# Attention with two banks for the transposes: the next scores go behind one transpose

## The chip, the cores and the metric

One NeuronCore of a Trainium2 chip runs the whole program. The metric is the device time of one execution in microseconds: the median of the runs before the change is 971.01 us (970.05 to 972.16, three runs).

## The reference

The program is three layers after each other, on float32 data. Only the first is touched by the change: attention with queries averaged in twos.

```python
# q, k, v: 4 x 8 heads x 1152 x 64
q_pool = q.reshape(B, H, S // 2, 2, D).mean(axis=3)          # 576 queries
scores = scale * np.matmul(q_pool, k.transpose(0, 1, 3, 2))  # 576 x 1152
scores = scores - np.max(scores, axis=-1, keepdims=True)
attn = np.exp(scores)
attn = attn / (np.sum(attn, axis=-1, keepdims=True) + 1e-09)
out = np.matmul(attn, v)
# then two gated layers of width 512 and 1024 over 4 x 576 rows (moe, moe2)
```

## The kernel before, in words

Attention works on 16 pairs of heads. A pair has 2 x 576 queries, cut into nine tiles of 128 rows: four whole tiles of each head and one mixed tile of the two rests of 64. The main loop (L630) has one turn, here called a place, for each tile; places are numbered 0 to 8 in a pair. In place s the program issues the exponential of tile s + 1, brings tile s of exponentials into the layout that the product with the values wants (keys on partitions), computes the scores of tile s + 2, and their maximum. The scores (`scores`, L286) are six matmuls of 128 x 384 into three PSUM banks of one of two buffers SC, the mixed tile nine (two 64 rows wide or fed by `qc`). The maximum (`smax`, L307) is one reduction on DVE, the exponential (`sexp`, L322) one ACTIVATE on ACT with the row sums as a second, small instruction. So SC[s % 2] passes from scores to maximum to exponential, and only then are its banks free.

There are two ways to turn a tile of exponentials, in pairs 1 to 14 (`quick`):
- Places 0 to 3, here called block places (`by_block`): one 32 x 32 block transpose on DVE into the tile BLK (`turn_blocks`, L361); after the fourth, 16 DMAs on the SP queue move the blocks into the tile E (`move_blocks`, L367). These are the near queries, 256 of each head.
- Places 4 to 8, here called turned places: nine 128 x 128 transposes on PE (`tfill`, L337). Six go into banks 1 and 2 of the tile's own scores buffer, which its exponential has just set free, three into a bank TX. Copies (`tcopy`, L391) bring them to the tile M, two of 384 columns on ACT and one on DVE. These are the far queries, 320.

Pairs 0 and 15 turn all nine tiles on PE. The value products (`pv_part`, L400) have a PSUM bank of their own, tag `pv`, and stand where the table `shares` (L346) puts them: it lists (place, number of key blocks), counted from the pair's place 0, so place 9 is place 0 of the next pair. The near products of an inner pair stand in places 8 and 9, the far ones in 10, 11 and 12. A float32 matmul of these shows in the trace as two instructions.

What else the engines do stands in tables of places as well. PREP lists POOL's cuts of q and k of the next pair into a high and a low part (`q_sum`, `q_own`, `k_hi`, `k_lo`), q's copy to the other half of the partitions on ACT (`q_double`), and the loads. The weights of the next layers come as 64-bit floats, 21 pieces in all, one in an even inner pair, two in an odd one; a piece goes through `conv_steps` (L107): load (SP), Abs (ACT, `mag`), clamp (POOL), three steps on the bits (DVE), high part (ACT), low part (POOL), store (SP). BITS says where the DVE steps stand. A step is recorded at one of three hooks of a place: `at_gap` (its start), `at_mid` (before the scores), `at` (its end). Each engine, and the SP queue, works in the order in which the program is written.

Of the kernel before, what the change touches and what calls it, by code (L numbers as in the profile page):

```python
# [11 lines left out]
F32 = mybir.dt.float32  # L12
F32R = mybir.dt.float32r
# [49 lines left out]
def attn_moe_kernel(ctx: ExitStack, tc: tile.TileContext, qT, kT, vP, muk, mur, wk, wv, wr, wth, wtr, wti, wch, ident, out):  # L63
# [94 lines left out]
    def attention(first):  # L158
# [97 lines left out]
        def k_hi(P):  # L256
            khs[P] = nat.tile([128, S], F32R, tag="kh", name="kh")
            cut_hi("pool", khs[P], raws[P])

        def k_lo(P, h, i):  # L260
            c = slice(SP * i, SP * i + SP)
            d, o = half[h], half[1 - h]
            if i == 0:
                t = kts[P, h] = kp.tile([128, S], F32R, tag="kt", name="kt")
                cut_hi("pool", t[d], raws[P][d])
            cut_lo("pool", kts[P, h][o, c], raws[P][d, c], khs[P][d, c])
# [124 lines left out]
        def tcopy(n, c):  # L391
            e = ("act", "act", "dve")[c] if quick(n // KT) else COPY[3 if n == 0 else 4 if n in (2, 4) else 2 if n % 18 in SHORT else n % 2][c]
            out = erow(n, c)
# [4 lines left out]
            bank(e, r, b)  # L398

        def pv_part(k, x):  # L400
# [106 lines left out]
        def start():  # L507
# [108 lines left out]
        assert next(pieces, None) is None  # L616
# [565 lines left out]
```

## Time and profile before

| what | value |
|---|---|
| median of three runs | 971.01 us |
| profiled execution | 972.1 us, span 970.3 us |
| PE busy | 922.6 us, 95% of the span |
| DVE, ACT, POOL busy | 691.5, 550.8, 612.8 us |
| attention's inner pairs (1 to 14) | about 38 to 446 us |
| granted PE clock, mean | 0.995 |

A time in the trace is counted from the start of the span. A row of the timeline may merge several instructions of one kind (x6), and its duration runs from the first one's start to the last one's end; ends of matmuls overlap the next start. What an engine can do is therefore best read from start to start.

### The profile page before, as it was taken

The numbers are of one execution on the slowest core, as the hardware profiler recorded it, in microseconds if no ns is written. First come the engines' busy times: TensorE is split into PE (matmuls) and PEld (weight loads), VectorE is DVE, ScalarE is ACT, GpSimd is POOL, SyncE is SP. The second block draws the span as 40 slices with busy tenths as digits, with TensorE's granted clock in tenths as the row PEclk, the third lists the DMA queues.
The fourth block names the chain that finished last, engine by engine and source line by source line (L and its number), as shares of the span: only waits on it lengthen the run. The fifth ranks groups of instructions, "written<-read, shape, count | busy, mean of one in ns | idle before, by whom it ended". The sixth has DMA issues, their size and how long they took to land.

```text
span 970.3 us, 17479 instructions
## 1 busy us (share of the span) xinstructions
PE 922.6 (95%) x6328; PEld 780.8 (80%) x6328; DVE 691.5 (71%) x974; ACT 550.8 (57%) x1131; POOL 612.8 (63%) x663
## 2 busy tenths in 40 slices
PE   7988999999999998998999899999999999999998
PEld 5766666666666666666898899999999999999998
DVE  6787888877888887784538888888646764575722
ACT  6767766677666668765556555646435433343410
POOL 7767877687786777773417556556536665574731
PEclk9999999999999999999999999999999999999999
DMA  8176757687575777645563333333402501010001
GB/s 260 56 205 166 221 194 224 191 269 205 164 225 184 236 209 229 181 126 156 187 212 105 101 103 95 99 94 122 161 2 98 185 2 50 1 44 7 25 26 49
DMA packets 60807, 132.65 MB, mean 137 GB/s; under 512 B 10736, under 2 KB 29872, under 8 KB 60720
## 3 DMA queue, kind: packets, MB, share of 16 engines
q1 hardware_dynamic: 60720, 131.53, 43.7%
q8 instruction: 50, 0.82, 0.4%
q14 instruction: 37, 0.30, 0.1%
HBM read 73.08 MB, written 24.79 MB: 101 GB/s over the span
## 4 chain that ended last, share of the span: by engine, by line
PE 59%; DVE 14%; ACT 9%; DMA 7%; SPq 5%; issue 3%; POOL 3%; DVEq 0%; ACTq 0%; POOLq 0%
PE ps L1074 12%; PE ps L826 9%; PE ps L807 9%; PE sc L297 6%; PE ps L1093 5%; PE pv L412 5%; PE ps L1020 5%; DVE m L318 5%; ACT e L330 5%; SPq L374 4%; PE sc L340 3%; PE ps L776 3%; DVE cv L141 2%; DVE blk L365 2%; ACT q L254 2%
## 5 line engine op out<-in xcount | busy, mean ns | idle before, releaser
L318 DVE TENSOR_REDUCE m<-sc 128x1 f32<-128x1152 f32 x138 | 186.1, 1348 | 66.6 <-PE sc L297 65.5
L330 ACT ACTIVATE e<-sc,m 128x1152 f32<-128x1152 f32 x144 | 176.2, 1224 | 71.3 <-DVE m L318 70.0
L297 PE MATMUL sc<-kt,q 128*128 128x384 f32 (+1 forms) x864 | 200.6, 358 | 8.1 <-ACT M L397 3.7
L297 PEld LDWEIGHTS sc<-kt,q 128*128 128x128 f32 (+1 forms) x864 | 142.1, 187 | 39.0 <-issue 19.8
L1074 PE MATMUL ps<-b,a 128*128 128x288 f32 x816 | 111.3, 296 | 0.0
L1074 PEld LDWEIGHTS ps<-b,a 128*128 128x128 f32 x816 | 109.4, 188 | 0.6
L807 PE MATMUL ps<-x,a 128*128 128x288 f32 x768 | 103.7, 295 | 2.5 <-DVE xt L831 2.5
L807 PEld LDWEIGHTS ps<-x,a 128*128 128x128 f32 x768 | 102.2, 188 | 2.8 <-DVE xt L831 2.7
L826 PE MATMUL ps<-k,b 128*128 128x288 f32 x768 | 103.4, 294 | 0.0
L826 PEld LDWEIGHTS ps<-k,b 128*128 128x128 f32 x768 | 102.0, 188 | 0.3
L340 PEld LDWEIGHTS sc<-idn,e 128*128 128x128 f32 x528 | 58.2, 143 | 49.2 <-ACT e L330 38.5
L340 PE MATMUL sc<-idn,e 128*128 128x128 f32 x528 | 78.2, 285 | 19.8 <-ACT e L330 19.8
L200 POOL TENSOR_TENSOR kt<-kn,kh 64x576 fp32r<-64x576 f32 (+1 forms) x64 | 90.6, 1436 | 2.2
L412 PE MATMUL pv<-M,vn 128*64 128x320 f32 x576 | 87.4, 440 | 0.0
L365 DVE STREAM_TRANSPOSE blk<-e 128x1152 f32<-128x1152 f32 x56 | 76.0, 1357 | 0.0
L412 PE MATMUL pv<-E,vn 128*64 128x256 f32 x576 | 70.3, 388 | 3.5 <-DMA E<-blk 3.1
L794 POOL TENSOR_TENSOR k<-h,k 128x288 fp32r<-128x288 f32 x64 | 56.7, 900 | 18.7 <-ACT k L793 17.4
L412 PEld LDWEIGHTS pv<-M,vn 128*64 128x64 f32 x576 | 37.4, 136 | 36.1 <-issue 11.3
L412 PEld LDWEIGHTS pv<-E,vn 128*64 128x64 f32 x576 | 39.6, 138 | 27.4 <-issue 10.0
L810 DVE TENSOR_TENSOR h<-h 128x288 f32<-128x288 f32 x64 | 38.1, 601 | 26.9 <-ACT h L809 26.6
L1038 ACT ACTIVATE q<-q 128x512 f32<-128x512 f32 x18 | 11.4, 632 | 79.3 <-DVE q L1035 79.3
L149 POOL TENSOR_TENSOR a<-a 128x192 fp32r<-128x192 f32 (+1 forms) x29 | 20.6, 709 | 56.5 <-ACT a L145 28.4
(138 smaller groups left out, 1747.6 us busy)
## 6 DMA issues: line engine op xcount, KB each, us to landing
E<-blk SPq DMA_DIRECT2D x224, 144.0 KB
vn<-vP SPq DMA_DIRECT2D x16, 576.0 KB
kn<-kT SPq DMA_DIRECT2D x15, 576.0 KB
qn<-qT SPq DMA_DIRECT2D x15, 576.0 KB
b<-wtk SPq DMA_DIRECT2D x9, 576.0 KB
rb<-scr SPq DMA_DIRECT2D x32, 144.0 KB
out<-xt SPq DMA_DIRECT2D x32, 144.0 KB
cv<-wk SPq DMA_DIRECT2D x8, 512.0 KB
```

Source lines behind the costliest of these rows:

```text
L200: engines[e].tensor_tensor(out, x, hi.bitcast(F32), ALU.subtract)
L297: r = pe.matmul(sc[0:m, c, 0:384], lhsT=x, rhs=k[:, 384 * c:384 * c + 384], start=(i == 0), stop=(i == len(ops) - 1),)
L318: r = dve.tensor_reduce(m, scs[n][:, :, 0:384], axis=AX.XY, op=ALU.max, negate=True)
L330: r = act.activation(e, sc[:, :, 0:384], AF.Exp, bias=m, scale=1.0, accum_out=rss[P][:, t:t + 1])
L340: r = pe.transpose(ps[:, 128 * j:128 * j + 128], es_[n][:, c, 128 * j:128 * j + 128], idn)
L365: dve.transpose(out, es_[n].rearrange("p a b -> p (a b)").rearrange("p (k m i) -> p k m i", k=KT, m=4))
L412: pe.matmul(out, lhsT=vns[P][:, h, j], rhs=e, start=(x == 0), stop=(x == KT - 1))
L794: pool.tensor_tensor(q[:, 1], h, q[:, 0].bitcast(F32), ALU.subtract)
L807: pe.matmul(ps, lhsT=WK[k, f // 4][:, w, 128 * (f % 4):128 * (f % 4) + 128], rhs=x[k][:, c], start=(k == 0 and n == 0), stop=(k == 3 and n ...
L826: pe.matmul(pss[d], lhsT=WV[f][:, w, 128 * d:128 * d + 128], rhs=k2[f][:, c], start=(f == 0 and n == 0), stop=(f == 7 and n == 2))
L1020: pe.matmul(ps, lhsT=y[k // 2][:, k % 2, x], rhs=WT[k][:, w], start=(k == 0 and p == 0), stop=(k == 3 and p == 2))
L1074: pe.matmul(pss[d], lhsT=zs[j][z][:, 128 * d:128 * d + 128], rhs=WTK[min(j, 8)][:, w, cs], start=(m == 0 and n == 0), stop=(m == 8 and n = ...
```

## The change

Transposes of the turned places go to two banks, TX and TY, and to bank 2 of the tile's scores buffer; TY is also the bank of the value products, which had `pv` before. Of a tile's nine key blocks, the last goes first, alone, into bank 2 ("o", copied by ACT); then come the scores of tile s + 2; then four blocks into TY ("y", copied by ACT at the start of the next place) and four into TX ("x", copied by DVE after the maximum). The tables of places change with it: value products in two near and two far parts, the bits of the weights in places 2 and 3, the preparation of q and k, Abs and the stores. An inner diff of the code and of one line of each table:

```diff
-PREP = ((0, 0, 'kh'), (0, 2, 'qs'), (0, 2, 'qo', 0), ..., (3, 1, 'qd', 0), ..., (3, 2, 'qd', 1), (4, 2, 'kl', 1, 0), (5, 1, 'kl', 1, 1), ...)
+PREP = ((-1, 2, 'qs'), (0, 0, 'qm'), (0, 0, 'qo', 0), ..., (2, 1, 'qd', 0), (2, 2, 'kt', 0), (3, 1, 'kt', 1), (3, 1, 'qd', 1), ..., (6, 2, 'kl', 1, 1), ...)
-BITS = (((8, 1), (8, 2), (9, 1)), ((2, 1), (3, 1), (8, 2)))
+PIECES = {"a": (((2, 1), (2, 2), (3, 1)), (9, 13, 15)), "b": (((3, 2), (11, 1), (11, 2)), (12, 14, 16)), "e": (((3, 1), (3, 1), (3, 2)), (9, 13, 15))}
...
+        TY = psV.tile([128, 512], F32, tag="ty", name="ty")
...
             if P == NP - 2:
-                return ((7, 2), (8, 7)), ((9, 5), (11, 4))
+                return ((8, 9),), ((9, 5), (11, 4))
...
-            return ((8, 4), (9, 5)), ((10, 3), (11, 3), (12, 3))
+            return ((9, 5), (10, 4)), ((11, 5), (12, 4))
...
+        FILL = {"o": (8, 9), "y": (0, 4), "x": (4, 8)}
+        def fill(n, w):
+            flat = es_[n].rearrange("p a b -> p (a b)")
+            k0, k1 = FILL[w]
+            ps = {"o": scs[n][:, 2], "x": TX, "y": TY}[w]
+            for j, k in enumerate(range(k0, k1)):
+                r = pe.transpose(ps[:, 128 * j:128 * j + 128], flat[:, 128 * k:128 * k + 128], idn)
...
+        def take(n, w):
...
+            e = "dve" if w == "x" else "act"
+            r = (act.copy if e == "act" else dve.tensor_copy)(out, ps)
...
             if x == 0:
-                pvs[k] = psV.tile([128, 320], F32, tag="pv", name="pv")
+                pvs[k] = TY
...
-            for bits, (i, piece) in zip(BITS[:1 + P % 2], pieces):
+            for kind, (i, piece) in zip("ab" if P % 2 else "e", pieces):
+                bits, (z, zl, zs) = PIECES[kind]
...
-                at_mid(base + 1, mag)
+                at_mid(base + (kind == "b"), mag)
...
-                at_mid(base + KT + 1, hi)
-                at(base + KT + 1, lo)
-                at_mid(base + KT + 3, store)
+                at_mid(base + z, hi)
+                at(base + zl, lo)
+                at_mid(base + zs, store)
...
+            take_rest()
             if quick(s // KT):
...
-                    for c in (1, 2, 0):
-                        tfill(s, c)
-                    tcopy(s, 1)
-                    tcopy(s, 2)
+                    fill(s, "o")
+                    take(s, "o")
                     sexp(s + 1)
-                    tcopy(s, 0)
...
             if s + 2 < NT:
                 scores(s + 2)
+            if quick(s // KT) and not by_block(s):
+                fill(s, "y")
+                fill(s, "x")
+                rest.append(s)
+            if s + 2 < NT:
                 smax(s + 2)
+            if quick(s // KT) and not by_block(s):
+                take(s, "x")
+                if s in plan:
+                    take_rest()
             run_pv(s)
```

On PE, in places 7 and 8 of an inner pair and 0 and 1 of the next (L340 are the transposes, L297 the scores, L412 the value products, whose key block counts twice, once for each head), there stands before:

```order
L340 MATMUL sc_120<-idn,e 128x128 x6
L340 MATMUL tx<-idn,e 128x128 x3
L297 MATMUL sc_120<-kt,q_0_0_123 128x384 x6
L340 MATMUL sc_121<-idn,e 128x128 x6
L340 MATMUL tx<-idn,e 128x128 x3
L297 MATMUL sc_121<-kt,q_0_0_123 128x384 x6
L412 MATMUL pv<-E,vn 64x256 x8
L297 MATMUL sc_120<-kt,q_0_1_124 128x384 x6
L412 MATMUL pv<-E,vn 64x256 x10
L297 MATMUL sc_121<-kt,q_0_1_124 128x384 x6
```

and now, in the same places (L412 are the transposes, L302 the scores, L446 the value products):

```order
L412 MATMUL sc_120<-idn,e 128x128
L302 MATMUL sc_120<-kt,q_0_0_124 128x384 x6
L412 MATMUL ty<-idn,e 128x128 x4
L412 MATMUL tx<-idn,e 128x128 x4
L412 MATMUL sc_121<-idn,e 128x128
L302 MATMUL sc_121<-kt,q_0_0_124 128x384 x6
L412 MATMUL ty<-idn,e 128x128 x4
L412 MATMUL tx<-idn,e 128x128 x4
L302 MATMUL sc_120<-kt,q_0_1_125 128x384 x6
L446 MATMUL ty<-E,vn 64x256 x10
L302 MATMUL sc_121<-kt,q_0_1_125 128x384 x6
L446 MATMUL ty<-E,vn 64x256 x8
```

Eight of nine transposes moved behind the scores, and the near value products moved by one place.

On DVE in an even pair, the bits (L133, L137, L141) stand before around its place 0, between maxima (L318) and the block transpose (L365):

```order
L133 TENSOR_SCALAR cv<-cv 128x512
L318 TENSOR_REDUCE m<-sc_121 128x1
L137 SCALAR_TENSOR_TENSOR cv<-cv 128x512
L141 SCALAR_TENSOR_TENSOR cv<-cv 128x512
L365 STREAM_TRANSPOSE blk<-e 128x9x4x32
L141 SCALAR_TENSOR_TENSOR cv<-cv 128x512
L318 TENSOR_REDUCE m<-sc_120 128x1
```

and now in its places 2 and 3 (maxima are L323, block transposes L370):

```order
L370 STREAM_TRANSPOSE blk<-e 128x9x4x32
L137 SCALAR_TENSOR_TENSOR cv<-cv 128x512
L323 TENSOR_REDUCE m<-sc_120 128x1
L141 SCALAR_TENSOR_TENSOR cv<-cv 128x512
L370 STREAM_TRANSPOSE blk<-e 128x9x4x32
L133 TENSOR_SCALAR cv<-cv 128x512
L137 SCALAR_TENSOR_TENSOR cv<-cv 128x512
L323 TENSOR_REDUCE m<-sc_121 128x1
L141 SCALAR_TENSOR_TENSOR cv<-cv 128x512
```

Nothing of the bits is left around place 0; five steps stand around the third and fourth block transpose.

On the SP queue, in an even pair, the stores of two finished pieces (L153, L154) stand before the norm's broadcast (rb) and the block moves (L374):

```order
L444 DMA scr<-rt 10x32 x4
L153 DMA wv_88<-cv 128x512
L154 DMA wv_88<-cv 128x512
L153 DMA wv_89<-cv 128x512
L154 DMA wv_89<-cv 128x512
L451 DMA rb<-scr 64x576 x2
L374 DMA E<-blk 32x1152 x16
L231 DMA vn<-vP 128x1152
L122 DMA cv<-wv 128x1024 x2
L223 DMA kn<-kT 128x1152
```

and now behind the moves (L379), ahead of the load of the values and of the next two pieces (L122):

```order
L478 DMA scr<-rt 10x32 x4
L485 DMA rb<-scr 64x576 x2
L379 DMA E<-blk 32x1152 x16
L153 DMA wv_88<-cv 128x512
L154 DMA wv_88<-cv 128x512
L153 DMA wv_89<-cv 128x512
L154 DMA wv_89<-cv 128x512
L232 DMA vn<-vP 128x1152
L122 DMA cv<-wv 128x1024 x2
L224 DMA kn<-kT 128x1152
```

The stores moved past the sixteen block moves and stand right ahead of the loads that use the same three buffers.

## Rows read from the trace of the kernel before

**Rows 1.** The page: busy us of each engine; one group, mean ns.

```profile
PE 922.6 (95%) x6328; PEld 780.8 (80%) x6328; DVE 691.5 (71%) x974; ACT 550.8 (57%) x1131; POOL 612.8 (63%) x663
...
L412 PE MATMUL pv<-M,vn 128*64 128x320 f32 x576 | 87.4, 440 | 0.0
```

**Rows 2.** Busy time of PE, PEld, DVE, ACT, POOL in a stretch of ten pairs.

```profile
124.60:412.80 288.20, 267.22 (x1742) 186.89 (x1741) 235.39 (x246) 204.25 (x351) 218.31 (x211) 1.00 0.69 209
```

**Rows 3.** Timeline (start us, us): exponentials of tile 0, pairs 4 and 14.

```profile
124.59 1.22 ACT L330 ACTIVATE e<-sc,m 128x1152 f32<-128x1152 f32 x1 [0.18 <-DVE m L318]
...
412.74 1.22 ACT L330 ACTIVATE e<-sc,m 128x1152 f32<-128x1152 f32 x1 [0.17 <-DVE m L318]
```

**Rows 4.** Timeline: one turned place, ACT, PE and DVE.

```profile
263.39 1.22 ACT L330 ACTIVATE e<-sc,m 128x1152 f32<-128x1152 f32 x1 [0.26 <-DVE m L318]
...
264.60 0.47 ACT L397 COPY M<-tx 128x384 f32<-128x384 f32 x1
264.75 0.87 PE L340 MATMUL sc<-idn,e 128*128 128x128 f32 x6 [0.33 <-ACT e L330]
...
265.71 1.32 PE L297 MATMUL sc<-kt,q 128*128 128x384 f32 x6
...
267.13 1.36 DVE L318 TENSOR_REDUCE m<-sc 128x1 f32<-128x1152 f32 x1 [0.78 <-PE sc L297]
...
268.58 1.23 ACT L330 ACTIVATE e<-sc,m 128x1152 f32<-128x1152 f32 x1 [0.17 <-DVE m L318]
```

**Rows 5.** Timeline of PE: place 8, then places 0 to 2 of the next pair.

```profile
269.98 1.95 PE L412 MATMUL pv<-E,vn 128*64 128x256 f32 x16 [0.36 <-PE sc L297]
271.86 1.33 PE L297 MATMUL sc<-kt,q 128*128 128x384 f32 x6
273.11 2.38 PE L412 MATMUL pv<-E,vn 128*64 128x256 f32 x20
275.42 1.32 PE L297 MATMUL sc<-kt,q 128*128 128x384 f32 x6
276.67 1.84 PE L412 MATMUL pv<-M,vn 128*64 128x320 f32 x12
278.44 0.44 PE L297 MATMUL sc<-kh,qc 128*128 128x384 f32 x1
...
280.22 1.84 PE L412 MATMUL pv<-M,vn 128*64 128x320 f32 x12
```

**Rows 6.** Timeline of ACT: q's copies in place 3; tile 2, even pair.

```profile
283.77 2.33 ACT L254 CAST q<-q 64x1152 fp32r<-64x1152 f32 x2
...
306.41 1.22 ACT L330 ACTIVATE e<-sc,m 128x1152 f32<-128x1152 f32 x1 [2.25 <-DVE m L318]
```

**Rows 7.** Timeline of DVE and POOL: bits in an even pair, then undisturbed ones.

```profile
299.62 1.97 POOL L200 TENSOR_TENSOR q<-qn,q 64x576 fp32r<-64x576 f32 x1
...
300.22 1.92 DVE L141 SCALAR_TENSOR_TENSOR cv<-cv 128x512 uint32<-128x512 uint32 x1
...
304.97 1.34 DVE L318 TENSOR_REDUCE m<-sc 128x1 f32<-128x1152 f32 x1
306.24 1.36 DVE L365 STREAM_TRANSPOSE blk<-e 128x1152 f32<-128x1152 f32 x1
...
283.27 0.65 DVE L137 SCALAR_TENSOR_TENSOR cv<-cv 128x512 uint32<-128x512 uint32 x1
```

**Rows 8.** SP's timeline; last, from the chain: a load's issue to landing.

```profile
256.61 10.09 SPq L374 DMA_DIRECT2D E<-blk  x16
266.80 0.53 SPq L231 DMA_DIRECT2D vn<-vP  x1
...
280.73 0.38 SPq L154 DMA_DIRECT2D wk<-cv  x1
...
294.14 4.58 DMA cv<-wv
```

**Rows 9.** Waits of the SP queue, 124 to 412 us: total, times, longest.

```profile
SPq L444 <- DVE rt L437: 109.0, 10, 13.6
```

More of the change, by code (lines that the diff above doesn't have):

```diff
@@ L46 @@
 NORM = 9
-PREP1 = ((1, 0, 'kh'), (1, 2, 'qs'), (2, 2, 'qo', 0), (3, 2, 'qo', 1), (4, 2, 'qd', 0), (3, 2, 'kl', 0, 0), (3, 2, 'kl', 0, 1), (5, 2, 'qd', 1), (4, 2, 'kl', 1, 0), (4, 2, 'kl', 1, 1), (5, 2, 'lk'), (5, 2, 'lq'), (17, 2, 'lv'))
-PREP = ((0, 0, 'kh'), (0, 2, 'qs'), (0, 2, 'qo', 0), (1, 1, 'qo', 1), (1, 1, 'lk'), (3, 1, 'qd', 0), (2, 0, 'lq'), (2, 2, 'kl', 0, 0), (3, 1, 'kl', 0, 1), (3, 2, 'qd', 1), (4, 2, 'kl', 1, 0), (5, 1, 'kl', 1, 1), (17, 2, 'lv'))
-BITS = (((8, 1), (8, 2), (9, 1)), ((2, 1), (3, 1), (8, 2)))
+PREP1 = ((1, 0, 'kh'), (1, 2, 'qs'), (1, 2, 'qm'), (2, 2, 'qo', 0), (3, 2, 'qo', 1), (4, 2, 'qd', 0), (3, 2, 'kt', 0), (3, 2, 'kl', 0, 0), (3, 2, 'kl', 0, 1), (5, 2, 'qd', 1), (4, 2, 'kt', 1), (4, 2, 'kl', 1, 0), (4, 2, 'kl', 1, 1), (5, 2, 'lk'), (5, 2, 'lq'), (17, 2, 'lv'))
+PREP = ((-1, 2, 'qs'), (0, 0, 'qm'), (0, 0, 'qo', 0), (0, 2, 'qo', 1), (1, 1, 'lk'), (1, 2, 'kh'), (2, 0, 'lq'), (2, 1, 'qd', 0), (2, 2, 'kt', 0), (3, 1, 'kt', 1), (3, 1, 'qd', 1), (4, 0, 'kl', 0, 0), (5, 0, 'kl', 0, 1), (6, 0, 'kl', 1, 0), (6, 2, 'kl', 1, 1), (17, 2, 'lv'))
+PIECES = {"a": (((2, 1), (2, 2), (3, 1)), (9, 13, 15)), "b": (((3, 2), (11, 1), (11, 2)), (12, 14, 16)), "e": (((3, 1), (3, 1), (3, 2)), (9, 13, 15))}
 F64_MIN = float(np.array([0x38000000], np.uint32).view(np.float32)[0])
@@ L236, in q_sum, with q_scale @@
             pool.tensor_tensor(t, t, x[:, 1], ALU.add)
+        def q_scale(P):
+            t = qs[P][:, 0]
             pool.tensor_scalar(t, t, 1.0 / 16.0, 1.0, op0=ALU.mult, op1=ALU.mult)
@@ L258, in k_hi, with k_top @@
             cut_hi("pool", khs[P], raws[P])
+        def k_top(P, h):
+            t = kts[P, h] = kp.tile([128, S], F32R, tag="kt", name="kt")
+            cut_hi("pool", t[half[h]], raws[P][half[h]])
         def k_lo(P, h, i):
@@ L262, in k_lo @@
             d, o = half[h], half[1 - h]
-            if i == 0:
-                t = kts[P, h] = kp.tile([128, S], F32R, tag="kt", name="kt")
-                cut_hi("pool", t[d], raws[P][d])
             cut_lo("pool", kts[P, h][o, c], raws[P][d, c], khs[P][d, c])
@@ L374, in move_blocks, with erow @@
                     sp.dma_start(out=E[32 * m:32 * m + 32, b], in_=BLK[32 * b:32 * b + 32, m])
-        def erow(n, c):
+        def erow(n, kk):
             P, x = n // KT, tile_of(n)
-            kk = slice(3 * c, 3 * c + 3)
             g = 0 if x and x[1] < 2 else 1
@@ L391, in tcopy @@
         def tcopy(n, c):
-            e = ("act", "act", "dve")[c] if quick(n // KT) else COPY[3 if n == 0 else 4 if n in (2, 4) else 2 if n % 18 in SHORT else n % 2][c]
-            out = erow(n, c)
+            e = COPY[3 if n == 0 else 4 if n in (2, 4) else 2 if n % 18 in SHORT else n % 2][c]
+            out = erow(n, slice(3 * c, 3 * c + 3))
             ps, b = turned(n, c)
@@ L398, in tcopy, with take_rest @@
             bank(e, r, b)
+        FILL = {"o": (8, 9), "y": (0, 4), "x": (4, 8)}
[5 more added lines that the diff above has]
+                r = pe.transpose(ps[:, 128 * j:128 * j + 128], flat[:, 128 * k:128 * k + 128], idn)
+                if w != "y":
+                    bank("pe", r, "tx" if w == "x" else (n % 2, 2))
+        def take(n, w):
+            k0, k1 = FILL[w]
+            out = erow(n, slice(k0, k1))
+            ps = {"o": scs[n][:, 2], "x": TX, "y": TY}[w][:, 0:128 * (k1 - k0)]
+            ps = ps.rearrange("p (a b) -> p a b", b=128) if tile_of(n) else ps.rearrange("p (a h b) -> p a h b", h=2, b=64)
+            e = "dve" if w == "x" else "act"
+            r = (act.copy if e == "act" else dve.tensor_copy)(out, ps)
+            if w != "y":
+                bank(e, r, "tx" if w == "x" else (n % 2, 2))
+        rest = []
+        def take_rest():
+            for n in rest:
+                take(n, "y")
+            rest.clear()
         def pv_part(k, x):
@@ L497, in run_pv @@
                 pv_part(*k)
-        steps = {"qs": q_sum, "qo": q_own, "qd": q_double, "kh": k_hi, "kl": k_lo, "lk": load_k, "lq": load_q, "lv": load_v}
+        steps = {"qs": q_sum, "qm": q_scale, "kt": k_top, "qo": q_own, "qd": q_double, "kh": k_hi, "kl": k_lo, "lk": load_k, "lq": load_q, "lv": load_v}
         def prep_sched(P):
@@ L512, in start @@
             w = w.bitcast(mybir.dt.bfloat16)
-            ps = psV.tile([128, 384], F32, tag="pv", name="warm")
+            ps = TY[:, 0:384]
             for _ in range(WARM):
```

## Prediction

> **What bounds the kernel now.** I read the page's first part, then the busy times of stretches, then the timeline of one pair of heads, engine by engine. The page [rows 1] puts PE at 95% of the span, which looks like nothing left to win. But the ten pairs from 124.6 to 412.8 us take 288.2 us, and PE is busy 267.2 of them, DVE 235.4, POOL 218.3, ACT 204.3 [rows 2]. So a pair lasts 28.8 us, and about 2 us of it PE stands still, by the profile's own count of busy. The exponentials' starts give the same pitch: tile 0 of pair 4 starts at 124.59, tile 0 of pair 14 at 412.74 [rows 3], 28.8 us a pair. Attention's 14 inner pairs are about 400 us of the run; nothing after 475 us is touched by the diff.
>
> Inside a pair there are two kinds of places, with different limits. In the turned places (4 to 8) the bound is a chain and no engine. One tile [rows 4]: the exponential starts at 263.39, its nine transposes at 264.75, the scores of the tile after next at 265.71, the maximum at 267.13, the exponential that needs it at 268.58. Two tiles alternate on this loop, so a place takes 5.19 / 2 = 2.60 us. PE's share of it is 0.96 us of transposes (264.75 to 265.71) and 1.25 us of scores (275.42 to 276.67, where nothing was waited for [rows 5]): 2.21 us. The rest, 0.39 us, is the wait.
>
> In the block places (0 to 3) PE works almost without a break. From start to start [rows 5]: the near value products of place 8 take 1.88 us (16 instructions), of place 0 2.31 us (20), scores 1.25 us, a far part 1.77 us (12), the mixed tile's scores 1.78 us. Here the disturbances come from DVE: the three steps on a weight's bits.
>
> **The change part by part.** *The loop of the turned places.* Only one transpose of nine now stands between exponential and next scores; the other eight come after the scores, into TY and TX. The loop becomes: exponential to transpose 1.36 us (263.39 to 264.75), one transpose 0.96 / 9 = 0.11, first score to maximum 1.42 (265.71 to 267.13), maximum to exponential 1.45 (267.13 to 268.58): 4.34 us for two tiles, 2.17 a place. What is late next is an engine. PE still needs 2.21. ACT: 1.21 from exponential to the next copy (263.39 to 264.60); a copy of 384 columns takes 0.47 and an exponential of 1152 1.22, so about 0.98 ns a column over a base of 0.10, which makes 0.22 for 128 columns and 0.60 for 512: 2.03. DVE: 1.36 for a maximum over 1152 columns, so 0.60 for 512 in proportion and some 0.7 with a base like ACT's: 2.06. All three lie within 0.2 us of each other, so I take PE's 2.21 plus a little for meeting edges, 2.25. Gain: 0.35 x 5 = 1.75 us a pair. The last bank of the scores waits for the small copy on ACT, which stands behind the copy of TY: 1.21 + 0.60 + 0.22 = 2.03 us after the exponential's start, while the fifth score of six would be due four sixths of 1.25 us after the first, at 1.36 + 0.11 + 0.83 = 2.30; that wait is hidden. Without this cover it would cost up to 0.6 us a place.
>
> *Value products in two near and two far parts.* The same 72 instructions: none now in place 8, 20, 16, 20 and 16 in places 0 to 3. A far part of 20 is 1.77 + 8 x 0.13 = 2.8 us, of 16 2.3 (0.13 is the pitch inside twelve: their 1.84 us less the 0.44 of one [rows 1], over eleven). PE's own times in places 0 to 3: 1.25 + 2.31, 1.25 + 1.88, 1.78 + 2.8, 1.25 + 2.3, together 14.8 us. With 5 x 2.21 for the turned places PE needs 25.9 us a pair, where 28.8 are spent now. So 2.9 us a pair is the most that can come, and the question is how much of it is given back.
>
> *Bits of the weights.* They leave places 8 and 0, where in even pairs they held up the maximum: the exponential of tile 2 at 306.41 had waited 2.25 us for it [rows 6]. They go to places 2 and 3, five steps in even pairs and four in odd ones. A step costs 0.65 us when POOL leaves it alone, and up to 1.92 when it starts while POOL is in a two-input operation: at 300.22 a step lasts until POOL's 1.97 us operation from 299.62 is over and half a microsecond more [rows 7]. DVE in places 0 to 3: eight operations at 1.27 us from start to start (304.97 to 306.24 [rows 7]), some 0.4 for the norm, five steps at just under 0.6: 13.4 us bare, against PE's 14.8. Each collision adds 0 to 1.3 us; POOL's queue in places 2 and 3 is now one-input cuts first and two-input ones after, so I take three collisions of 0.65 us, 1.9 us, of which the difference of 1.4 hides all but 0.5 in even pairs, and all in odd ones. Bounds: 0 and 2.5.
> The Trainium skill ("SBUF — State Buffer", section "SBUF: two separate sides") says that a DVE operation with two SBUF inputs and a GpSimd operation exclude each other for the whole instruction. The 1.92 us agree; by that rule alone, were all five steps to meet a 1.4 us operation, the stretch would be at the upper bound, six even pairs 2 us longer each, and the time at 954.
>
> *Loads, stores, Abs.* For the first piece of a pair Abs moves from place 1 to place 0 on ACT, where the exponential of tile 2 is queued behind it, and that releases a scores buffer. The load is still issued in place 8, but on SP it now stands behind the stores, which moved behind the 16 block moves, and its buffer is the one being stored. From the end of the fourth block transpose: 16 moves take 10.2 us of issuing (256.61 to 266.80), two stores 0.8 or four 1.6 (0.38 each and a little between), the load of the values 0.53, then the load; a load landed 4.58 us after its issue [rows 8]. Now SP has 10.9 us a pair in which it waits for the norm's transpose (109.0 us in 10 waits) [rows 9]; these hide the added wait for the stores, but not Abs' early place. Walking the places with the times above, the fourth transpose ends 14 to 15 us after the end of tile 8's exponential, the piece lands at 31 to 33, and Abs (0.67) would have been due at 30; the exponential behind it has 1.3 us of slack. Cost: nothing before an even pair, 0.7 us before an odd one (two pieces, four stores). Bounds: 0 and 4, the upper if stores and load land one after the other, 4.6 us each.
>
> *Other edits.* q's copies (2.33 us together) move on ACT from place 3, where the exponential of tile 5 stood behind them [rows 6], to places 2 and 3, one each; I count this within the 2.9 us. POOL does the same work in another order; its 218.3 / 10 = 21.8 us fit into 26. The values and TY share a bank: the first far product waits for ACT's copy of the near ones, 0.4 us, behind the mixed scores (1.78 us), so hidden.
>
> Sum per pair: 28.8 - 25.9 = 2.9, less 0.2 for the edges of the turned places (0.04 x 5), less 0.6 (the mean of 0.5 and 0.7): 2.1 us. Pairs 1 to 13: 27.3 us; pair 14 only its turned places, 1.75. Together 29 us. The profiled execution took 972.1 us (its span 970.3 and 1.8 around it), 1.1 over the median of the runs; 972.1 - 29 = 943 for such an execution, 942 as a median.
>
> **The rivals.** *Far less comes: the edges cost.* Three engines at 2.03 to 2.21 us in one loop, each waiting for the next, settle at 2.4 rather than 2.25, and collisions and Abs cost 1.2 us a pair instead of 0.6. Then a pair gains 2.1 - 0.75 - 0.6 = 0.75, and the time is 971 - 13 x 0.75 - 1 = 960. For it: nothing in the trace runs so tightly; against: the block places do, at PE's pace.
> *Slower: the loop through SP.* Tile 2's exponential, fourth block transpose, 16 moves, stores, load, Abs, tile 2's exponential of the next pair: from the exponential to the transpose's end DVE has three block transposes and two maxima (1.27 each), the norm (0.4) and two steps of bits (0.6 each), 8.1 us with the last one's end, and with two collisions 9.9; the moves 10.3; stores and load one after the other 0.4 + 4.6 + 4.6; Abs 0.7. That is 28.7 to 30.5 us, a mean of 29.6 against the 28.8 now: 13 x 0.8 = 10 us slower, 981. It decides when the first piece lands more than 3 us after Abs' turn. For it: both waits are new; against: a move's end and a store's overlap, and SP has 10.9 us to spare.
> *All comes.* The stalls vanish in slack elsewhere: 971 - 13 x 2.8 - 2 = 933, which is about 930 with pair 14's block places too.
> *The change does not do what it says*: the chain stays, because the small copy on ACT is late each time (0.6 us a place, above) and eats the 0.35: about 970.
>
> **How the numbers follow.** Forecast 942: 0.5, with its own range 934 to 951. Edges: 0.22 (951 to 967). All: 0.13 (926 to 934). No change: 0.05. Loop through SP: 0.1. The range 928 to 962 leaves out about 2 in 10. A measurement of this kernel tells 0.2%, 2 us, from no change; faster 0.86, same 0.04, slower 0.1.
>
> **What would show it.** In a turned place the starts of exponentials 2.2 to 2.3 us apart, one transpose, six scores, eight transposes on PE without a gap; PE's busy share of the inner pairs near 97%; the exponential of tile 2 in even pairs no longer 2 us in wait for its maximum; in places 2 and 3 bits of 0.65 us beside some of 1.7; ACT waiting for a weight's load before Abs in place 0 of odd pairs, by about 2 us. Wrong: places 4 to 8 still at 2.5 or more; waits of over 3 us for the load in each pair; PE waiting in place 0 for the block moves.

## The result and the profile after

The change takes 941.43 us (938.5 to 944.02, four runs), the kernel before 970.53 us (969.09 to 972.16) beside it: a ratio of 0.9699, with a 95% interval of 0.9661 to 0.9737. The forecast of 942 us and its sign hold. The sum behind it holds less well than the total: pairs 1 to 13 bring 2.9 us less than forecast, and what follows them some 4.5 us more.

The page of the changed kernel, busy us of each engine as in [rows 1]:

```profile
PE 906.5 (97%) x6328; PEld 784.2 (84%) x6328; DVE 698.8 (75%) x974; ACT 541.9 (58%) x1131; POOL 610.9 (65%) x663
```

Ten pairs in one stretch (busy PE, PEld, DVE, ACT, POOL, as in [rows 2]), from tile 0's exponential of pair 4 to that of pair 14, which are the two rows of the timeline below it (start us, us, as in [rows 3]):

```profile
115.90:386.90 271.00, 258.91 (x1742) 190.92 (x1742) 243.37 (x246) 197.98 (x351) 216.99 (x211) 1.00 0.75 222
```

```profile
115.83 1.22 ACT L335 ACTIVATE e<-sc,m 128x1152 f32<-128x1152 f32 x1 [0.17 <-DVE m L323]
...
386.76 1.23 ACT L335 ACTIVATE e<-sc,m 128x1152 f32<-128x1152 f32 x1 [0.18 <-DVE m L323]
```

A pair takes 27.1 us, not 28.8. PE counts as busy for 25.9 of them and stands still for 1.2 us, where 0.8 was predicted (26.7 a pair). The granted clock is 1.00, its upper level of 2.4 GHz, as before, so nothing comes from it.

A turned place of an odd pair, PE, ACT and DVE, which answers to [rows 4]:

```profile
326.04 1.23 ACT L335 ACTIVATE e<-sc,m 128x1152 f32<-128x1152 f32 x1
...
327.40 0.33 PE L412 MATMUL sc<-idn,e 128*128 128x128 f32 x1
327.49 1.29 PE L302 MATMUL sc<-kt,q 128*128 128x384 f32 x6
327.77 0.27 ACT L423 COPY M<-sc 128x128 f32<-128x128 f32 x1
...
328.19 1.22 ACT L335 ACTIVATE e<-sc,m 128x1152 f32<-128x1152 f32 x1 [0.16 <-DVE m L323]
328.62 0.60 PE L412 MATMUL ty<-idn,e 128*128 128x128 f32 x4
328.88 1.36 DVE L323 TENSOR_REDUCE m<-sc 128x1 f32<-128x1152 f32 x1 [0.19 <-PE sc L302]
329.05 0.60 PE L412 MATMUL tx<-idn,e 128*128 128x128 f32 x4
329.56 0.33 PE L412 MATMUL sc<-idn,e 128*128 128x128 f32 x1
...
330.34 1.22 ACT L335 ACTIVATE e<-sc,m 128x1152 f32<-128x1152 f32 x1 [0.15 <-DVE m L323]
```

Two places take 330.34 - 326.04 = 4.30 us, 2.15 each. PE's order is the predicted one: one transpose from 327.40, scores from 327.49, TY's four from 328.62, TX's four from 329.05, the next tile's at 329.56, 2.16 us later. The profile shows no idle time of PE here, and yet it is still the chain that sets the pace: exponential to transpose 1.36 us (326.04 to 327.40), transpose to first score 0.09, first score to maximum 1.39 (327.49 to 328.88), maximum to exponential 1.46 (328.88 to 330.34), together 4.30. PE alone is faster, as the same work in an even pair shows, where nothing is waited for:

```profile
300.00 1.29 PE L302 MATMUL sc<-kt,q 128*128 128x384 f32 x6
301.12 0.60 PE L412 MATMUL ty<-idn,e 128*128 128x128 f32 x4
301.56 0.60 PE L412 MATMUL tx<-idn,e 128*128 128x128 f32 x4
...
302.02 1.29 PE L302 MATMUL sc<-kt,q 128*128 128x384 f32 x6
```

From scores to scores PE needs 2.02 us. In the odd pair it is held up for some 0.1 us a place, which the ends of its matmuls cover in the count of busy time.

What is given back stands in the block places, and in even pairs also in the first turned place. ACT's timeline of an even pair (10), then of an odd one (11), which answer to the last row of [rows 6]:

```profile
284.42 0.67 ACT L126 ACTIVATE cv<-cv 128x512 f32<-128x512 f32 x1 [3.10 <-issue]
...
313.07 0.66 ACT L126 ACTIVATE cv<-cv 128x512 f32<-128x512 f32 x1 [4.07 <-DMA cv<-wv]
```

Abs stands still for 3.10 and 4.07 us, and the exponential of tile 2 right behind it. In the first row the profile names no releaser ("issue"); the SP queue below shows that its load is late there too. On PE the mixed tile's scores need that exponential's buffer; the last line is PE's wait for it from 120 to 390 us (us in total, times, longest):

```profile
286.35 0.44 PE L302 MATMUL sc<-kh,qc 128*128 128x384 f32 x1 [0.81 <-ACT e L335]
...
299.11 0.66 PE L412 MATMUL tx<-idn,e 128*128 128x128 f32 x4 [0.51 <-DVE M L423]
...
314.98 0.44 PE L302 MATMUL sc<-kh,qc 128*128 128x384 f32 x1 [1.90 <-ACT e L335]
...
PE sc L302 <- ACT e L335: 8.9, 8, 1.9
```

That is 1.0 us in an even pair and 0.8 in an odd one, on average of pairs 4 to 13. PE's wait is that of Abs less some 2.2 us: 2.28 us of Abs give none, 3.10 give 0.81, 4.07 give 1.90.

The SP queue ahead of these two Abs (the last answers to [rows 8]):

```profile
276.87 0.49 SPq L232 DMA_DIRECT2D vn<-vP  x1
279.50 0.33 SPq L122 DMA_DIRECT2D cv<-wv  x1
...
304.95 0.56 SPq L154 DMA_DIRECT2D wv<-cv  x1
305.60 0.56 SPq L232 DMA_DIRECT2D vn<-vP  x1
306.63 2.04 SPq L122 DMA_DIRECT2D cv<-wv  x2
```

and what SP waits for from 120 to 390 us (us in total, times, longest), as [rows 9]:

```profile
SPq L478 <- DVE rt L471: 38.3, 10, 4.6
...
SPq L122 <- DMA wk<-cv: 12.4, 8, 2.2
SPq L122 <- DMA wv<-cv: 6.6, 6, 2.1
```

In the even pair SP stands 2.1 us between the values' load (over at 277.36) and the weight's load at 279.50. There are 14 such waits of a load (L122) for a store, 19.0 us in all; the wait for the norm's transpose (L478), the slack in which the forecast hid them, shrank from 109.0 to 38.3 us. In the odd pair the first Abs starts 313.07 - 306.63 = 6.4 us after its load's issue; [rows 8] had 4.58.

The other part is on DVE, an even pair, as [rows 7]:

```profile
291.86 0.38 DVE L133 TENSOR_SCALAR cv<-cv 128x512 uint32<-128x512 uint32 x1
292.26 1.79 DVE L137 SCALAR_TENSOR_TENSOR cv<-cv 128x512 uint32<-128x512 uint32 x1
...
295.25 1.94 DVE L141 SCALAR_TENSOR_TENSOR cv<-cv 128x512 uint32<-128x512 uint32 x1
```

Two steps on the bits take 1.79 and 1.94 us, beside POOL's two-input operations, and the 0.51 us for which PE waits at 299.11 is for the copy of TX that stands behind them on DVE. Even pairs take 27.7 us and odd ones 26.5, on average of pairs 4 to 13.

### The profile page after: what moved, and what is told of

It reads as the page before. It is cut to its first block, busy times and chain, and to the rows that moved or that the text cites. A ratio compares the mean times of both kernels' runs of the same rounds, so it can differ in the third digit from the quotient of the medians.

```text
span 937.8 us, 17502 instructions
## 1 busy us (share of the span) xinstructions
PE 906.5 (97%) x6328; PEld 784.2 (84%) x6328; DVE 698.8 (75%) x974; ACT 541.9 (58%) x1131; POOL 610.9 (65%) x663
## 4 chain that ended last, share of the span: by engine, by line
PE 65%; DVE 9%; POOL 9%; DMA 7%; ACT 5%; issue 3%; SPq 2%; POOLq 0%; ACTq 0%; DVEq 0%
PE ps L1116 12%; PE ps L868 9%; PE ps L849 9%; PE sc L302 8%; PE ty L446 7%; PE ps L1135 5%; PE ps L1062 5%; PE ps L818 3%; ACT e L335 2%; POOL kt L201 2%; DVE m L323 2%; DMA cv<-wk 2%; DVE blk L370 2%; DMA cv<-wv 1%; POOL q L201 1%
## 5 line engine op out<-in xcount | busy, mean ns | idle before, releaser
L323 DVE TENSOR_REDUCE m<-sc 128x1 f32<-128x1152 f32 x138 | 186.0, 1348 | 35.0 <-PE sc L302 33.7
L302 PE MATMUL sc<-kt,q 128*128 128x384 f32 (+1 forms) x864 | 192.5, 351 | 4.7 <-DMA kt<-kh 2.5
L302 PEld LDWEIGHTS sc<-kt,q 128*128 128x128 f32 (+1 forms) x864 | 146.1, 189 | 24.3 <-issue 12.2
L201 POOL TENSOR_TENSOR kt<-kn,kh 64x576 fp32r<-64x576 f32 (+1 forms) x64 | 95.7, 1508 | 3.2
L370 DVE STREAM_TRANSPOSE blk<-e 128x1152 f32<-128x1152 f32 x56 | 76.5, 1366 | 11.3 <-ACT e L335 11.2
L446 PE MATMUL ty<-M,vn 128*64 128x320 f32 x576 | 84.6, 438 | 0.0
L446 PE MATMUL ty<-E,vn 128*64 128x256 f32 x576 | 69.2, 385 | 0.3 <-ACT M L423 0.3
L446 PEld LDWEIGHTS ty<-M,vn 128*64 128x64 f32 x576 | 38.5, 136 | 36.1 <-issue 7.2
L446 PEld LDWEIGHTS ty<-E,vn 128*64 128x64 f32 x576 | 38.5, 136 | 24.5 <-issue 7.8
L1092 POOL TENSOR_TENSOR q<-t,q 128x256 f32<-128x256 f32 x32 | 24.5, 787 | 48.9 <-ACT q L1082 48.9
L818 PE MATMUL ps<-x,blk 128*128 128x288 f32 x384 | 54.5, 301 | 1.8 <-POOL x L798 1.1
```

What stands on the lines that cost most here:

```text
L201: engines[e].tensor_tensor(out, x, hi.bitcast(F32), ALU.subtract)
L302: r = pe.matmul(sc[0:m, c, 0:384], lhsT=x, rhs=k[:, 384 * c:384 * c + 384], start=(i == 0), stop=(i == len(ops) - 1),)
L323: r = dve.tensor_reduce(m, scs[n][:, :, 0:384], axis=AX.XY, op=ALU.max, negate=True)
L370: dve.transpose(out, es_[n].rearrange("p a b -> p (a b)").rearrange("p (k m i) -> p k m i", k=KT, m=4))
L446: pe.matmul(out, lhsT=vns[P][:, h, j], rhs=e, start=(x == 0), stop=(x == KT - 1))
L818: pe.matmul(pss[d], lhsT=WR[k][:, w, 128 * d:128 * d + 128], rhs=x[k][:, c], start=(k == 0 and n == 0), stop=(k == 3 and n == 2))
```

## The experiments

Theory A: the gain is the chain of the turned places, and what is missing to PE's own time is Abs' wait for its load. B: the tables carry the gain. C: what is missing are the collisions of bits with POOL. Further letters are explained where they stand in the expectations. The kernel before took 969.01, 969.02 and 970.34 us beside the runs; each ratio is to it, with its 95% interval.

**turn_only.** Before, with the new transposes (`fill`, `take`, TY) and the old tables; pair 14's near products in place 8.

```diff
+        FILL = {"o": (8, 9), "y": (0, 4), "x": (4, 8)}
...
-                return ((7, 2), (8, 7)), ((9, 5), (11, 4))
+                return ((8, 9),), ((9, 5), (11, 4))
```

> The kernel before, with only the new transposes (one block, scores, four blocks into TY, four into TX); all tables of places as before, but the near products of pair 14 all in place 8. Theory A (the chain in the turned places is what the change takes away): turned places fall from 2.60 to about 2.2 us, 5 x 0.4 = 2.0 us a pair, 13 pairs, so 945 us, up to 952 where the bits in places 8 and 0 hold it back. Theory B (the tables carry the gain, the transposes are only put elsewhere): 962 to 971 us, turned places still at 2.5 or more.

955.69 us, ratio 0.9893 (0.9834 to 0.9952). The turned places do run at 2.15 us, but the step from tile 0's exponential to tile 1's grows from 2.60 to 2.86, and tile 1 to tile 2 takes 6.2 to 6.6 us in pairs of both kinds, where before took 6.6 in even pairs and 4.2 to 5.2 in odd ones. PE, ACT and DVE at that place, between pairs 8 and 9:

```profile
258.43 1.95 PE L442 MATMUL ty<-E,vn 128*64 128x256 f32 x16 [1.88 <-DMA E<-blk]
```

```profile
263.99 0.38 ACT L452 COPY xt<-ty 128x256 f32<-128x256 f32 x1 [4.71 <-PE ty L442]
264.26 1.23 ACT L331 ACTIVATE e<-sc,m 128x1152 f32<-128x1152 f32 x1
```

```profile
261.12 1.68 DVE L141 SCALAR_TENSOR_TENSOR cv<-cv 128x512 uint32<-128x512 uint32 x1
262.72 1.34 DVE L319 TENSOR_REDUCE m<-sc 128x1 f32<-128x1152 f32 x1
```

The faster places bring PE to place 8 before the moved blocks are there, so the near products wait 1.88 us, and ACT stands 4.71 us in front of its copy of them. The exponential behind the copy could hardly have come sooner all the same: its maximum is over at 264.06, at the end of a stretch from 255.53 on in which DVE never rests and three steps on the bits take 4.3 us. So the bits in places 8 and 0 bind here, as the expectation allowed, with the wait for the blocks beside them. The new transposes alone keep less than half of the gain.

**tables_only.** After, with the old transposes (six in the scores' banks, three in TX, all ahead of the scores).

```diff
-                    fill(s, "o")
-                    take(s, "o")
+                    for c in (1, 2, 0):
+                        tfill(s, c)
+                    tcopy(s, 1)
+                    tcopy(s, 2)
                     sexp(s + 1)
+                    tcopy(s, 0)
```

> The changed kernel with the old transposes (nine before the next scores, six of them in the scores' own banks); all tables of places are the new ones. Theory A: turned places stay at 2.6 us; the block places get at most 1 us a pair from the bits that left places 8 and 0, and lose some of it to Abs in place 0: 958 to 968 us. Theory B: 941 to 950 us.

957.62 us, ratio 0.9892 (0.9863 to 0.9922). The turned places stay at 2.60 us, as they must. The gain is in the front places: tile 1 to tile 2 takes 3.1 us on average, where before took 4.5 in odd pairs and 6.6 in even ones. Neither half is the change: 13 and 11 us alone, 29 together, and both halves contain the edit of pair 14. In pairs 1 to 13 the profiled executions gain 13.8 us with the transposes, 5.2 with the tables and 24.4 with both. B falls, and A is not the whole either.

**shares_only** and **pv_old.** The first is before with the new places of the value products, the second after with the old ones.

```diff
-            return ((8, 4), (9, 5)), ((10, 3), (11, 3), (12, 3))
+            return ((9, 5), (10, 4)), ((11, 5), (12, 4))
```

> The kernel before with only the value products of the inner pairs in their new places (none in place 8, near ones in 0 and 1, far ones in 2 and 3). Theory A (alone they only move PE's work, the chain of the turned places and the bits around place 0 stay): 964 to 972 us. Theory E (their old places were a bound of their own): 955 to 962 us.

> The changed kernel with the value products of the inner pairs in their old places (near ones in places 8 and 0, far ones in three parts), pair 14's near ones left in place 8. Theory A (PE's own sum per pair sets the pace, 25.7 us where nothing waits): the same instructions, one part and some 0.25 us of switching more a pair, 942 to 946 us. Theory E (the new places keep PE fed while DVE and ACT are busy): 950 us or more, with PE waiting in places 0 and 1.

shares_only: 976.82 us, ratio 1.0064 (1.0041 to 1.0086), slower by 0.6%. pv_old: 955.52 us, ratio 0.9858 (0.9829 to 0.9888), 14 us over the change. So the same edit costs 6 us on the old transposes and is worth 14 on the new ones. In pv_old the turned places keep their 2.15 us, and tile 1 to tile 2 takes 5.8 to 8.3. Two of its waits from 120 to 390 us (us in total, times, longest), then ACT and PE in pair 9:

```profile
ACT cv L126 <- DMA cv<-wv: 20.1, 5, 5.6
...
PE ty L446 <- ACT xt L456: 8.3, 7, 1.9
...
267.76 0.66 ACT L126 ACTIVATE cv<-cv 128x512 f32<-128x512 f32 x1 [4.86 <-DMA cv<-wv]
...
268.75 1.84 PE L446 MATMUL ty<-M,vn 128*64 128x320 f32 x12 [1.19 <-ACT xt L456]
```

The near and the far products share the bank TY. With the old places the far ones start one place earlier, and PE waits 8.3 us for ACT's copy of the near ones, which stands on ACT behind Abs and its late load. In shares_only the exponentials wait 71.7 us for maxima from 120 to 410 us (69 waits; in ten pairs of before, 44.2 us in 55 waits), and even pairs take 30.1 to 30.4 us, where before took 29.4; what makes those maxima late was not followed further.

**y_first.** After, with TY's four transposes ahead of the next scores: five in front of them and not one.

```diff
+            if quick(s // KT) and not by_block(s):
+                fill(s, "y")
             if s + 2 < NT:
                 scores(s + 2)
             if quick(s // KT) and not by_block(s):
-                fill(s, "y")
                 fill(s, "x")
```

> The changed kernel with the four transposes into TY ahead of the next scores, so five of nine stand in the chain instead of one. Theory A (the chain sets the pace of the turned places): each transpose in it costs 0.108 us, 0.43 us a loop of two tiles, 0.22 us a place, 5 places, 14 pairs: 15 us slower than the change, about 956 us. Theory D (PE's own time sets it, so the order on PE is nothing): 941 us.

954.78 us, ratio 0.9859 (0.9833 to 0.9885). The places now alternate, 3.0 and 2.1 us, 2.57 on average: nearly the old 2.60, and what theory A forecast; D falls. What stands between exponential and scores is what sets the place, and 13 us hang on four short transposes.

**abs_late.** After, with Abs of every piece in place 1, as before the change.

```diff
-                at_mid(base + (kind == "b"), mag)
+                at_mid(base + 1, mag)
```

> The changed kernel with Abs of every piece back in place 1 (for the first piece of a pair it was in place 0). Theory A (Abs waits for its load in front of tile 2's exponential, and PE waits behind it before the mixed tile's scores, 1.90 us in one odd pair and 0.81 in one even pair): those waits go, 1.35 us a pair, 13 pairs, 17 us: about 924 us. Theory C (what is given back is collisions of DVE's bits with POOL, the wait for Abs is slack): 938 to 942 us, and PE's waits turn up in places 3 and 4 instead.

937.14 us, ratio 0.9671 (0.9635 to 0.9708): 4 us better than the change in the median, and the two intervals overlap. In its profiled execution the ten pairs from tile 0 of pair 4 to tile 0 of pair 14 take 262.1 us, 26.2 a pair, and PE no longer waits before the mixed tile's scores. By A the whole 1.35 us a pair would have come back. In odd pairs Abs still waits for its loads, now ahead of tile 3, but mostly that costs nothing: pair 11 waits 0.55 us twice and takes 25.64 us; where the two waits are over 2 us together (pairs 7 and 13) PE loses 0.3 and 0.9. What is left stands in even pairs: 26.66 us in pairs 4, 8 and 10, and Abs waits for no load in any of these. POOL and DVE in pair 10, and DVE's one wait for a clamp from 120 to 376 us (us in total, times, longest):

```profile
285.80 1.40 POOL L201 TENSOR_TENSOR kt<-kn,kh 64x576 fp32r<-64x576 f32 x1
286.10 1.65 DVE L141 SCALAR_TENSOR_TENSOR cv<-cv 128x512 uint32<-128x512 uint32 x1
...
287.68 1.37 DVE L370 STREAM_TRANSPOSE blk<-e 128x1152 f32<-128x1152 f32 x1
...
DVE cv L133 <- POOL cv L129: 0.5, 1, 0.5
```

The step on the bits meets a two-input operation on POOL, and the fourth block transpose, right behind it on DVE, starts 12.86 us into the pair.

**no_bits** and **bits_next.** Both from abs_late: the first leaves the three DVE steps on the bits of attention's pieces out, the second puts them into places 0 to 2 of the next pair.

```diff
-                for (o, hook), step in zip(bits, cuts):
-                    (at_gap, at_mid, at)[hook](base + o, step)
```

```diff
-PIECES = {"a": (((2, 1), (2, 2), (3, 1)), (9, 13, 15)), ...}
+PIECES = {"a": (((9, 2), (10, 1), (10, 2)), (11, 13, 15)), ...}
```

> The changed kernel with Abs in place 1 for all pieces, and without the three steps on the bits of the weights' pieces during attention; this part of the computation is left out. Theory C (what is still given back with Abs late is the bits meeting POOL's operations, 26.3 us a pair against the 25.65 of the best pairs): all pairs at 25.65, 8 us under the kernel with Abs late alone, 924 to 930 us. Theory F (it is ACT and the loads): within 2 us of that kernel, 931 to 937 us.

> The changed kernel with Abs in place 1 for all pieces, and the bits a pair later, in places 0 to 2 of the next pair, where POOL stands still for about 3 us in front of the clamp; the high part moves to place 2. If the collisions are what is left (theory C): 927 to 934 us, under the kernel with Abs late alone. If DVE has no room in places 0 to 2 (theory G): 940 us or more, and exponential 2 late again.

no_bits: 924.23 us, ratio 0.9529 (0.9497 to 0.956), 25.6 to 26.0 us a pair from pair 4 on, although Abs still waits for its loads, up to 1.9 us a pair. bits_next: 947.51 us, ratio 0.9781 (0.9746 to 0.9815), slower than the change: theory G, and C's 927 to 934 is missed. The late exponentials are those of tile 3 in odd pairs (5.9 to 7.0 us after tile 2) and of tile 4 in even ones. The first run speaks for C and doesn't prove it: without the steps DVE is rid of the collisions, of the steps' own time, and of a wait for a late clamp, though the 0.5 us above leave little to that last one.

**abs_2.** After, with Abs and clamp of every piece in place 2, and the bits of an odd pair's first piece in place 3, where those of an even pair's piece stand already. The bits keep their number. Their neighbours on POOL change, since the clamp comes a place later in POOL's queue.

```diff
-PIECES = {"a": (((2, 1), (2, 2), (3, 1)), (9, 13, 15)), ...}
+PIECES = {"a": (((3, 1), (3, 1), (3, 2)), (9, 13, 15)), ...}
...
-                at_mid(base + (kind == "b"), mag)
-                at(base + 1, clamp)
+                at_mid(base + 2, mag)
+                at(base + 2, clamp)
```

> The changed kernel with Abs and clamp of all pieces in place 2, and the bits of the first piece of a pair in place 3. Theory A (ACT still waits for loads in place 1 with Abs there): exponential 3 of odd pairs comes 1 us earlier than with Abs in place 1, 0.4 us a pair, 930 to 934 us. Theory C (collisions are the rest, and more steps in place 3 meet more of them): 937 to 943 us, with exponential 5 or 6 later.

928.9 us (925.26 to 932.36, five runs), ratio 0.9572 (0.9545 to 0.9599): faster than both kernels, by 12 us than the change. A stretch of 264.1 us in its inner pairs:

```profile
115.90:380.00 264.10, 262.67 (x1784) 196.29 (x1782) 250.87 (x252) 204.31 (x362) 218.15 (x216) 1.00 0.79 235
```

PE is busy 262.67 of 264.10 us, and Abs never waits for a load. From pair 2 to pair 13 every pair takes 25.73 to 25.91 us, 25.8 on average. Are the collisions gone? The steps of the two kernels from 116 to 380 us (busy us, mean ns | idle before), first the change, then abs_2:

```profile
L137 DVE SCALAR_TENSOR_TENSOR cv<-cv 128x512 uint32<-128x512 uint32 x15 | 21.2, 1411 | 0.2
L141 DVE SCALAR_TENSOR_TENSOR cv<-cv 128x512 uint32<-128x512 uint32 x15 | 16.0, 1068 | 0.0
L133 DVE TENSOR_SCALAR cv<-cv 128x512 uint32<-128x512 uint32 x15 | 5.9, 396 | 0.0
```

```profile
L137 DVE SCALAR_TENSOR_TENSOR cv<-cv 128x512 uint32<-128x512 uint32 x15 | 19.7, 1316 | 0.3
L133 DVE TENSOR_SCALAR cv<-cv 128x512 uint32<-128x512 uint32 x15 | 15.1, 1004 | 0.0
L141 DVE SCALAR_TENSOR_TENSOR cv<-cv 128x512 uint32<-128x512 uint32 x15 | 10.2, 678 | 0.0
```

The steps take 43.1 us there and 45.0 here, as much as before. But these totals hide where they stand. The five steps of an even pair take 5.9 us in the change, 5.8 in abs_late and 4.6 in abs_2; the four of an odd pair take 2.7, 3.6 and 4.4. The same place in an even pair (10) as above, now in abs_2:

```profile
285.32 0.68 DVE L141 SCALAR_TENSOR_TENSOR cv<-cv 128x512 uint32<-128x512 uint32 x1
285.84 0.64 POOL L129 TENSOR_SCALAR cv<-cv 128x512 f32<-128x512 f32 x1 [3.58 <-ACT cv L126]
285.92 1.37 DVE L370 STREAM_TRANSPOSE blk<-e 128x1152 f32<-128x1152 f32 x1
```

POOL is only at the clamp, the step takes 0.68 us and not 1.65, and the block transpose starts 11.90 us into the pair, 0.96 earlier. The collisions have moved to odd pairs, where DVE has one step less and nothing is lost. So both theories hold in part. Of the 1.3 us a pair by which the change is longer than abs_2 (27.1 to 25.8), 0.9 go with Abs' wait for its load (27.1 to 26.2, abs_late) and 0.4 with the collisions of even pairs (26.2 to 25.8). The second share rests on these rows and on no_bits: abs_2 moves Abs, clamp and collisions at once, and no run moves the collisions alone. In the profiled execution of abs_2 (932.36 us, the longest of the five) pairs 0 and 1 take 30.7 and 28.3 us, where the change takes 27.95 and 25.99. Pair 0 takes 26.3 to 30.7 us in seven kernels that schedule it alike, so its time says nothing of an edit; why pair 1 is longer is open.

**bits_old, prep_old, loads_first.** After, each with one edit: the weights' pieces where they were before; the places of the cuts of q and k as before; on SP the weights' loads ahead of the values' load.

```diff
-                at_mid(base + (kind == "b"), mag)
+                at_mid(base + 1, mag)
...
+BITS = (((8, 1), (8, 2), (9, 1)), ((2, 1), (3, 1), (8, 2)))
```

```diff
-PREP = ((-1, 2, 'qs'), (0, 0, 'qm'), (0, 0, 'qo', 0), ...)
+PREP = ((0, 0, 'kh'), (0, 2, 'qs'), (0, 2, 'qm'), ...)
```

```diff
-                at(base - 1, load)
+                at_mid(base - 1, load)
```

> The changed kernel with the weights' pieces treated as before: bits in places 8 and 0 (and 2, 3, 8 for the second piece), Abs in place 1, stores ahead of the block moves. Theory A: the maximum of tile 2 waits behind two steps again, 6 us from exponential 1 to 2 in pairs of both kinds, about 1 us a pair slower than the change: 948 to 955 us. Theory C (the collisions in places 2 and 3 cost as much as those around place 0): 938 to 943 us.

> The changed kernel with the preparation of q and k in its old places (q's copies on ACT both in place 3, k's cuts in places 2 to 5). Theory A (POOL and ACT have room for either order, the value products and the transposes are what counts): 939 to 945 us. Theory H (the 2.3 us of q's copies ahead of exponential 5, or k's cuts, are part of the gain): 948 us or more, with the exponential of tile 5 later than now.

> The changed kernel with the loads of the weights' pieces ahead of the load of the values on the SP queue. Theory A (Abs in place 0 waits for a load that stands behind stores and values): the load lands 0.5 to 1.5 us earlier, PE's wait before the mixed scores shrinks, 0.4 to 0.8 us a pair, 931 to 937 us. If the load waits only for the stores to land, and the values' load costs it nothing: 940 to 943 us.

bits_old: 940.87 us, ratio 0.9716 (0.9682 to 0.9751). prep_old: 944.95 us, ratio 0.9728 (0.9693 to 0.9762). loads_first: 938.64 us, ratio 0.9663 (0.964 to 0.9686). All three intervals overlap the change's, so none of these edits is told from nothing, and A's 948 to 955 for bits_old is missed. (In loads_first's profiled execution odd pairs take 25.9 us, in the change 26.5; even ones take 27.7 in both.) Of bits_old this says something all the same: the pieces' new places give no measurable gain. They remove the wait for the maximum and put Abs' wait there instead: in bits_old the exponentials wait for maxima 54.8 us from 120 to 390 us, in the change 20.1, and tile 1 to tile 2 takes 5.5 us on average in both.

## Why the prediction was right

The forecast said that 2.9 us a pair can come and 0.8 are given back. By the ten pairs it is 3.0 (28.8 to abs_2's 25.8) and 1.3, so the mechanism is there, and 1.7 us a pair came where 2.1 were forecast. That the total is met within 1 us is luck in part: pair 14 made up for it.

*The loop of the turned places*: right in its chain, wrong in what binds. 2.25 us was forecast, 2.15 measured in odd pairs (1.89 to 2.41 in even ones, after a first step of 2.92 to 3.14 beside the bits). The forecast's chain of 4.34 us for two tiles, 2.17 a place, stands in the rows as 4.30, link by link. It was set aside for PE's 2.21, which is 2.02 in the rows, and the allowance for meeting edges wasn't needed. The small copy on ACT is over at 328.04, before the scores need their last bank, as forecast. y_first confirms the chain: four more transposes of 0.11 us for each of two tiles make 5.18 us, 2.59 a place, and 2.57 were measured.

*PE's sum*: right as a number. 25.9 us a pair was called the least that PE needs; abs_2 reaches 25.8 and no_bits 25.6, with the turned places at the chain's 2.15 us (14.8 + 5 x 2.15 = 25.6).

*Loads, stores, Abs*: the term that was mis-sized. It said nothing before an even pair and 0.7 us before an odd one. PE's stalls there are 0.81 and 1.90 us in the two pairs shown, and 1.0 and 0.8 on average in even and odd pairs: the odd term was right, the even one missing. I let the transfer of the stores end under other work; the rows show SP standing for it up to 2.2 us at a time, and 6.4 us from issue to Abs in the other. Also, the four tenths that each turned place gains fall away from the load's time. tables_only fits that: with places of 2.60 us, the same Abs in place 0 holds up little (tile 1 to 2 in 2.5 us in five of ten pairs, 3.1 on average; in the change 5.5). The sentence on the rival, that it decides once the piece lands over 3 us late, was right in kind; PE waits once Abs does for over 2.2 us, but in a pair that has got shorter elsewhere.

*Bits*: the durations are as forecast (1.79 and 1.94 us, up to 1.92 was said). The Trainium skill ("SBUF — State Buffer", "SBUF: two separate sides") says of such a pair that whoever starts first holds the port for its whole instruction; the 1.79 us step from 292.26 agrees, beside a POOL operation of 1.64 us from 291.87. The upper bound by that rule, 2 us an even pair, did not come. The forecast had 0.5 us in an even pair and nothing in an odd one; pairs 4, 8 and 10 of abs_late take 0.9 more than those of abs_2, and odd pairs lose nothing to collisions. So the reason given, DVE's room in an even pair, fits, and the size was 0.4 us short.

*Value products*: the step was wrong. I counted them as moved work at equal cost, and looked only at what a part takes on PE. pv_old shows them to be worth 14 us beside the new transposes and Abs in place 0: the wait of the first far product for ACT's copy of the near ones, which the forecast called hidden behind the mixed scores, is hidden in the new places alone. In turn_only the near products in place 8 also wait 1.88 us for the blocks.

*Pair 14*: wrong, and it hid the miss in the other pairs. I gave it 1.75 us. From the exponentials' starts, pairs 14 and 15 gain 6.3 us net, since 14's near products no longer wait in place 7 and its front places are shorter (tile 1 to 2 in 3.10 us, not 6.60). Pairs 1 to 13 gain 24.4 us (from 374.5 to 350.1), where 27.3 were forecast; pair 0 gives 1.6, within what it differs by from kernel to kernel anyway. That is 32.3 of the 32.6 us between the two profiled executions.

*The rivals*: "All comes" was given 933 and 0.13; one more shift of Abs, and it is there (928.9). "Edges" isn't seen in an odd pair's turned places, but its 1.2 us a pair for collisions and Abs are nearer to the 1.3 measured than the forecast's 0.6. The loop through SP is present as a wait, and smaller than priced. "Does not do what it says" is out, at 2.15 us a place.

## What to carry to other kernels

Where two edits are each worth little, run both halves: here the transposes bring 13 us, the tables 11, the two 29, and one of the tables alone makes the old kernel slower. When a loop gets faster, a load that was timed to it gets late; follow the in-order queues from the waiting instruction (here load, Abs, exponential, scores). Leaving work out removes its own time and its waits with it, so it can't tell these apart. Moving the work can, but compare it pair by pair: a total that stays (43 and 45 us of bits) can hide that collisions went from pairs without room to pairs that have it. And an engine that shows no idle time may still be following a chain; add up the chain's links from start to start before calling it the bound.

## What the runs showed of the hardware

The lone step with one input (L133), 0.38 us alone, also grows beside POOL. In abs_2, DVE:

```profile
316.41 1.52 DVE L133 TENSOR_SCALAR cv<-cv 128x512 uint32<-128x512 uint32 x1
```

POOL had a two-input operation of 1.69 us running from 315.96, and the step ends 0.28 us after it; the mean of fifteen went from 396 ns in the change to 1004 in abs_2, whose tables place it differently. I had expected this of the two-input steps only.

Transposes of 128 x 128 that follow each other take little: four, then the next kind, from 328.62 to 329.05, 0.11 us each.
